# Linear attention into an ELU feed-forward: three steps of round four moved or recast (two decayed states to ScalarE, one decayed query sooner, two more ELU steps in SBUF form)

## The chip, the cores and the metric

The kernel runs on one core of one Trainium2 chip. The metric is device time in microseconds; less is better. One core has TensorE (matmuls, PE in the profile), VectorE (DVE), ScalarE (ACT), GpSimd (POOL) and SyncE (SP, here only a queue of DMA issues). Matmul results go to PSUM; everything else lies in SBUF.

## The reference, cut to what matters

Linear attention with a decay per head over q, k, v of shape 4 batches x 8 heads x 768 positions x 64, in blocks of 64 positions. Its output, laid out as 3072 rows of 512, goes through two matrix products with an ELU between them.

```python
for b in range(nb):                                   # 12 blocks of 64 positions
    intra = (qb @ kb.T) * Dmask                       # Dmask[i, j] = lam ** (i - j), causal
    out[:, :, sl] = intra @ vb + (qb * lam_pow) @ kv_state
    kv_state = lam_block * kv_state + (kb * rev_pow).T @ vb
h = x @ w_in                                          # 512 -> 2048
g = where(h > 0, h, exp(min(h, 0)) - 1)               # ELU
return g @ w_out                                      # 2048 -> 512
```

Inputs and the result are float32; the kernel works in float16 between them, with float32 sums in PSUM.

## The kernel before, in words

**Blocks.** Work is cut into 24 blocks numbered s = 0 to 23: block s is one step of 64 positions for a pair of batches, so blocks s and s - 2 are neighbours in time of the same pair. For a block the kernel makes: the decayed values vd (L191), the decayed state sd (L200: the state of block s - 2 times lam to the 64th, per head), the decayed queries qs (L209), the masked scores P (L217), the output cast xt (L252) and the new state st (L264: what PSUM holds plus sd). The transposed keys and queries T of blocks 10 and later come from two DMA transposes on SP's queue (`dma_T`, L234 to L243, tile TD, two buffers; the tile of block 13 is that of block 11, so its transposes wait until the scores and the decayed queries of block 11 have read it). qs has two buffers and sd three.

**A visit.** `visit` (L278) is the attention work of TensorE for several blocks at once: the visit of block s takes qs and the state to the inter-block part of block s (L304), the scores of block s + 1 (L328, from T), the state update of block s (L320, from vd) and the product with P of block s (L313). Then DVE makes P of block s + 1 and st of block s, and ACT casts the output of block s to xt.

**Rounds.** From round 3 on, a loop over rounds grp = 3 to 11 (L601) with eight steps u = 0 to 7 each sets the order. A step issues one feature product `mm1_h` (L377, L385: 16 matmuls for 256 rows, into one of two PSUM buffers psH) that is written H(grp,u) below. Blocks 2 grp + 2 and 2 grp + 3 are visited in steps 1 and 5, so round 4 visits blocks 10 and 11 and round 5 blocks 12 and 13. After a feature product comes a part of the second product of an earlier round (`part`, L508, or `mm2`, L452). The second product of round 3 and later is a Strassen-like scheme in seven products, whose sums of g are made by `g_sum` on DVE (L490), and whose one leftover weight sum is `w_sum(3, 1)` in step (5,0) (L478).

**The ELU.** `elu` (L420) has two forms. The SBUF form (`mm1_e`, `mm1_g`): ACT makes e = exp(psH) (L395) and r = relu(psH) in float16 (L397), and DVE makes g = min(e - 1, r) from these two (L402); the last reader of psH is ACT. The PSUM form: ACT makes r = relu(-psH) (L429) and e = exp(-r) (L431), and DVE makes g = max(e - 1, psH) (L432); the last reader of psH is DVE. Round 3 and steps 0 to 4 of round 4 take the SBUF form. Below, g(grp,u) is DVE's instruction of a step in either form.

**Order.** The schedule is written by hand: every engine runs its instructions in the order in which the program issues them, and only semaphores hold one back. The loads of k, q and v of a later block (L70, two DMA issues each) stand in POOL's queue, in steps 0 and 4 of a round. From block 12 on, POOL also makes qs and sd, in steps 1 and 5 (`decay_q(s + 1, ...)`, `decay_s(s + 1, ...)`, L616 and L617). For block 11 the loop does this on DVE apart: sd in step (4,2) after st of block 10 (L654), and qs in step (4,3) after vd of block 11 (L656).

Of the kernel before, what the change touches and what calls it, by code (L numbers as in the profile page):

```python
# [11 lines left out]
AF = mybir.ActivationFunctionType  # L12
# [4 lines left out]
def kernel(  # L17
# [10 lines left out]
    nc = tc.nc  # L28
# [3 lines left out]
    NPR = B // 2  # L32
    NHP = H // 2
# [134 lines left out]
    lamL = cst.tile([128, NHP], FP32, name="lamL")  # L168
    powi = cst.tile([128, NHP, L], FP32, name="powi")

    st = [dict() for _ in range(NS)]
    state = {}
# [23 lines left out]
    def decay_s(s, eng):  # L196
        if not NPR <= s < NS - NPR:
            return
        st[s]["sd"] = asb.tile([128, 2, NHP, D], FP32, tag="sd", bufs=3, name=f"sd{s}")
        eng.tensor_tensor(  # L200
            out=st[s]["sd"][:], in0=state[s - NPR][:],
            in1=lamL[:].unsqueeze(1).unsqueeze(3).broadcast_to([128, 2, NHP, D]), op=ALU.mult,
        )

    def decay_q(s, eng):
        if not NPR <= s < NS:
            return
        st[s]["qs"] = asb.tile([128, NHP, 2, L], FP16, tag="qs", bufs=2, name=f"qs{s}")
        eng.tensor_tensor(  # L209
            out=st[s]["qs"][:], in0=st[s]["T"][:, 1],  # L210
            in1=powi[:].unsqueeze(2).broadcast_to([128, NHP, 2, L]), op=ALU.mult,
        )
# [32 lines left out]
    def att_X(s, eng):  # L245
        g, hf = divmod(s, 2)
        if g not in xt:
            xt[g] = asb.tile([128, NHP, 256], FP16, tag="xt", bufs=3, name=f"xt{g}")
        to = xt[g][:, :, hf * 128 : (hf + 1) * 128].rearrange("p y (r t) -> p r y t", r=2)
        O = st[s].pop("O").rearrange("p r (y t) -> p r y t", y=NHP)  # L250
        if eng is nc.scalar:
            nc.scalar.copy(out=to, in_=O)  # L252
        else:
            eng.tensor_copy(to, O)
# [122 lines left out]
    def mm1_h(grp, c0, nc_, n0, step=1):  # L377

        T = nc_ * 128
        nb = 512 // T  # L380
        name = f"{grp}_{c0}_{n0}"
        psH = ps.tile([128, nb, T], FP32, tag="h", bufs=2, name=f"psH{name}")
        for i, n in enumerate(features(nb, n0, step)):
            for kk in range(NHP):
                nc.tensor.matmul(  # L385
                    psH[:, i, :], lhsT=wi[n // 4][:, kk, (n % 4) * 128 : (n % 4 + 1) * 128],
                    rhs=xt[grp][:, kk, c0 * 128 : c0 * 128 + T],
                    start=(kk == 0), stop=(kk == NHP - 1),
                )
        unit[grp, c0, nc_, n0] = (psH, nb, T, name)  # L390

    def mm1_e(grp, c0, nc_, n0):
        psH, nb, T, name = unit[grp, c0, nc_, n0]
        e = msb.tile([128, nb, T], FP32, tag="e", bufs=4, name=f"e{name}")
        nc.scalar.activation(e[:], psH[:], AF.Exp)  # L395
        r = msb.tile([128, nb, T], FP16, tag="r", bufs=4, name=f"r{name}")
        nc.scalar.activation(r[:], psH[:], AF.Relu)  # L397
        unit[grp, c0, nc_, n0] = (e, r, nb, T, name)

    def mm1_g(grp, c0, nc_, n0, step=1):  # L400
        e, r, nb, T, name = unit.pop((grp, c0, nc_, n0))
        nc.vector.scalar_tensor_tensor(  # L402
            out=place(grp, c0, nc_, n0, nb, step), in0=e[:], scalar=-1.0, in1=r[:],
            op0=ALU.add, op1=ALU.min,
        )

    def place(grp, c0, nc_, n0, nb, step=1):

        if grp not in gel:
            gel[grp] = msb.tile([128, NF2, 2, 256], FP16, tag="g", bufs=4, name=f"g{grp}")  # L410
        cols = slice(c0 * 128, (c0 + nc_) * 128)
        if step > 1:
            return gel[grp][:, n0, :, cols]
        return gel[grp][:, n0 % NF2 : n0 % NF2 + nb, n0 // NF2, cols]
# [5 lines left out]
    def elu(grp, u):  # L420

        psH, nb, T, name = unit[grp, 0, 2, u]
        if grp == 3 or grp == 4 and u < 5:
            mm1_e(grp, 0, 2, u)
            mm1_g(grp, 0, 2, u, NF2)
            return

        r = msb.tile([128, nb, T], FP32, tag="r", bufs=4, name=f"r{name}")
        nc.scalar.activation(r[:], psH[:], AF.Relu, scale=-1.0)  # L429
        e = msb.tile([128, nb, T], FP32, tag="e", bufs=4, name=f"e{name}")  # L430
        nc.scalar.activation(e[:], r[:], AF.Exp, scale=-1.0)  # L431
        nc.vector.scalar_tensor_tensor(  # L432
            out=place(grp, 0, 2, u, 2, NF2), in0=e[:], scalar=-1.0, in1=psH[:],
            op0=ALU.add, op1=ALU.max,
        )
# [11 lines left out]
    def mm2(s, n0):  # L447
        if n0 == 0:
            acc[s] = M[nacc[0] % 2][:]
            nacc[0] += 1  # L450
        for n in range(n0, n0 + 4):
            nc.tensor.matmul(  # L452
                acc[s], lhsT=g_of(s, n), rhs=wo[n // 4][:, n % 4, :],
                start=(n == 0), stop=(n == NFT - 1),
            )
# [145 lines left out]
    for grp in range(3, NG):  # L601
        old, new = grp - 2, grp - 1
        for u in range(8):
            mm1_h(grp, 0, 2, u, NF2)
            s = 2 * grp + 2 + u // 4
            if s < NS and u % 4 == 0:

                if nload < NS:
                    load("k", nload)
                    load("q", nload)  # L610
                if nload <= NS:
                    load("v", nload - 1)
                    nload += 1
            if s < NS and u % 4 == 1:
                if s != 10:
                    decay_q(s + 1, nc.vector if s < 10 else nc.gpsimd)  # L616
                    decay_s(s + 1, nc.vector if s < 10 else nc.gpsimd)  # L617
                visit(
                    s, s if s < NS - NPR else None, s + 1 if s + 1 < NS else None,
                    s + 2 if s + 2 < NT else None,  # L620
                )
                dma_T(s + 3)

            if (grp, u) in five:
                mm2(5, 4 * five.index((grp, u)))
            end = grp == NG - 1
            if old >= 3 and u in (0, 2):
                part(old, {0: 3, 2: 7}[u])
            if new >= 3:
                at_u = {1: 2, 3: 4, 4: 1, 5: 5, 6: 6, 7: 3} if end else {3: 2, 4: 1, 5: 4, 6: 5, 7: 6}  # L630
                if u in at_u:
                    part(new, at_u[u])

            if old >= 3 and u == 1:
                add(old, 0, hi, res[old]["A"][:, hi], "p35")
                store(2 * old, res[old][0], slice(0, DM))
            if old >= 3 and u == 0:
                g_sum(old, 3)
            if new >= 3 and u in (4, 5, 6):
                g_sum(new, {4: 1, 5: 2, 6: 4}[u])  # L640
            if end and u == 3:
                g_sum(new, 3)
            if new >= 3 and u == 4:
                add(new, 0, lo, res[new]["A"][:, hi], "p2")
            if s + 1 < NS:
                if u % 4 == 1:
                    att_P(s + 1)
                if u % 4 == 2:
                    att_C(s + 2)
                    att_N(s)  # L650
                if u in (3, 7) and grp > 3:
                    decay_v(s + 1, nc.vector)
                if (grp, u) == (4, 2):
                    decay_s(s + 1, nc.vector)  # L654
                if (grp, u) == (4, 3):
                    decay_q(s + 1, nc.vector)  # L656
            if old >= 3 and u == 2:
                c2(old)
            if (grp, u) == (5, 0):
                w_sum(3, 1)  # L660
            elu(grp, u)
            if grp == 3 and u in (3, 6):
                decay_v(s + 1, nc.vector)
            if s < NS and u % 4 == 1:
                att_X(s, nc.scalar)
            if old >= 3 and u == 0:
                keep(old, "p35", res[old]["B"][:, hi])
            if new >= 3 and u == (1 if end else 3):
                keep(new, "p2", res[new]["B"][:, lo])
            if new >= 3 and u == (5 if end else 6):  # L670
                keep(new, "c45", res[new]["B"][:])
            if end and u == 6:
                keep(new, "u2", res[new]["A"][:, hi], 1)
            if end and u == 7:
                add(new, 0, hi, res[new]["B"][:, hi], "u2")
                store(2 * new, res[new][0], slice(0, DM))
            if (grp, u) == five[-1]:
                mm2_o(5)
# [58 lines left out]
```

## Time and profile before

| what | value |
|---|---|
| device time, three runs | median 210.2 us (210.11 to 211.47) |
| profiled execution | 210.27 us, of which the span is 208.5 us |
| busy, share of the span | PE 190.2 us (91%), DVE 172.1 (83%), ACT 140.7 (68%), POOL 132.0 (63%) |
| granted TensorE clock | full in all 40 slices |
| length of rounds, H(grp,0) to H(grp+1,0) | 5: 14.69 us, 6: 14.70, 7: 15.00, 8: 14.70 |

Times in the rows are microseconds from the start of the span; a row of the timeline has start, duration, engine, line, operation, output <- inputs, shapes, count, and in brackets the idle time of the engine just before it with what ended that. Matmul durations overlap, so for TensorE starts are compared, not durations. DVE's and ACT's durations also overlap a little: a DVE instruction of 0.68 us is followed by the next 0.60 us after its start. Spans on POOL are rough.

### The profile page before, as it was taken

The page shows a single profiled execution, that of the slowest core. Times are in us where ns is not written, and L with a number is a line of the kernel's source. Part 1 is how long each engine was busy: PE and PEld are TensorE (multiplying, and loading weights), DVE is VectorE, ACT ScalarE, POOL GpSimd, SP SyncE. Part 2 cuts the span into 40 slices and gives each one's busy share as a digit, 9 for nine tenths or more (in the row PEclk, how much of TensorE's full clock was granted, in tenths as well). Part 3 has the DMA queues.
Part 4 walks back from the last instruction along what each step waited for, and adds up shares of the span by engine and source line. Part 5 has one row for each costly group of instructions (what it writes and reads, how often), then busy time and mean ns, then how long its engine had stood idle before and what let it go on. Part 6 is the DMA issues. An engine that isn't in the chain of part 4 may idle for free.

```text
span 208.5 us, 7848 instructions
## 1 busy us (share of the span) xinstructions
PE 190.2 (91%) x3352; PEld 158.1 (76%) x3352; DVE 172.1 (83%) x281; ACT 140.7 (68%) x265; POOL 132.0 (63%) x180
## 2 busy tenths in 40 slices
PE   0448989999999999989999999999999999999991
PEld 0347977846776777868888888888888888888880
DVE  3677596798989898999989999999979956758672
ACT  5314686741784878767878778778788688877820
POOL 8978933899899879964999999999412200000000
PEclk9999999999999999999999999999999999999999
DMA  6999999999999999999999999999924404004043
GB/s 103 145 152 134 169 200 196 179 118 170 109 148 153 168 115 162 114 74 108 126 170 90 151 163 72 190 116 91 189 29 57 101 0 105 5 6 94 3 101 101
DMA packets 99731, 24.38 MB, mean 117 GB/s; under 512 B 92400, under 2 KB 96752, under 8 KB 99696
## 3 DMA queue, kind: packets, MB, share of 16 engines
q0 software_dynamic: 78208, 13.38, 96.0%
q1 hardware_dynamic: 20128, 10.03, 25.5%
q10 hardware_dynamic: 1360, 0.46, 1.2%
q8 instruction: 26, 0.43, 0.8%
q14 instruction: 9, 0.07, 0.1%
HBM read 27.27 MB, written 6.29 MB: 161 GB/s over the span
## 4 chain that ended last, share of the span: by engine, by line
PE 83%; DVE 6%; POOL 3%; DMA 3%; issue 2%; ACT 1%; DVEq 0%; POOLq 0%
PE psH L385 40%; PE psM L508 22%; PE psM L452 10%; DMA wi<-in_moe_w_in_dram 3%; PE psO_None L304 2%; PE psZ L328 2%; POOL vn L70 1%; DVE g L432 1%; PE psO_None L313 1%; PE psHA L508 1%; PE psHB L508 1%; PE psZ L320 1%; DVE s L490 1%; DVE vd L191 1%; DVE P L217 1%
## 5 line engine op out<-in xcount | busy, mean ns | idle before, releaser
L385 PE MATMUL psH<-xt,wi 128*128 128x256 f16 (+1 forms) x960 | 101.8, 257 | 2.6 <-DMA wi<-in_moe_w_in_dram 1.7
L385 PEld LDWEIGHTS <-wi 128*128 128x128 f16 x960 | 80.7, 101 | 13.7 <-issue 2.7
L432 DVE SCALAR_TENSOR_TENSOR g<-e,psH 128x512 f16<-128x512 f32 x59 | 40.2, 682 | 12.5 <-ACT e L431 12.1
L429 ACT ACTIVATE r<-psH 128x512 f32<-128x512 f32 x59 | 35.2, 597 | 21.5 <-PE psH L385 21.4
L431 ACT ACTIVATE e<-r 128x512 f32<-128x512 f32 x59 | 37.2, 630 | 1.9
L70 POOL DMA_DIRECT2D qn<-in_q_dram x46 | 32.4, 727 | 5.3 <-issue 2.7
L70 POOL DMA_DIRECT2D vn<-in_v_dram x48 | 34.0, 734 | 2.6 <-DMA qn<-in_q_dram 1.0
L395 ACT ACTIVATE e<-psH 128x512 f32<-128x512 f32 x37 | 22.2, 599 | 19.1 <-PE psH L385 18.8
L70 POOL DMA_DIRECT2D kn<-in_k_dram x46 | 32.5, 725 | 2.3 <-DMA wo<-in_moe_w_out_dram 2.3
L508 PEld LDWEIGHTS <-s 128*128 128x128 f16 x288 | 28.1, 98 | 3.4
L402 DVE SCALAR_TENSOR_TENSOR g<-e,r 128x512 f16<-128x512 f32 x37 | 26.1, 713 | 5.2 <-ACT r L397 5.2
L209 POOL TENSOR_TENSOR qs<-TD,powi 128x512 f16<-128x512 f16 x12 | 15.8, 1316 | 17.3 <-PE psO_None L304 12.4
L508 PE MATMUL psM<-wt,s 128*128 128x256 f16 x192 | 24.9, 273 | 0.0
L452 PE MATMUL psM<-wo,g 128*128 128x512 f16 x96 | 23.9, 380 | 0.0
L508 PEld LDWEIGHTS <-g 128*128 128x128 f16 x216 | 20.5, 98 | 2.6
L397 ACT ACTIVATE r<-psH 128x512 f16<-128x512 f32 x37 | 22.1, 598 | 0.0
L191 DVE TENSOR_TENSOR vd<-vn,rev 128x512 f16<-128x512 f16 x22 | 19.6, 891 | 0.0
L217 DVE TENSOR_TENSOR P<-psZ,mask 128x512 f16<-128x512 f32 x24 | 16.4, 684 | 2.6 <-PE psZ L328 2.0
L508 PE MATMUL psM<-wo,g 128*128 128x256 f16 x136 | 17.6, 273 | 0.0
L252 ACT CAST xt<-psO_None 128x512 f16<-128x512 f32 x20 | 11.5, 577 | 6.2 <-PE psO_None L313 6.2
L264 DVE TENSOR_TENSOR st<-psZ,sd 128x512 f16<-128x512 f32 x20 | 13.7, 683 | 0.9 <-PE psZ L320 0.9
L200 POOL TENSOR_TENSOR sd<-st,lamL 128x512 f32<-128x512 f16 x10 | 13.4, 1345 | 1.4 <-DVE st L264 1.4
(77 smaller groups left out, 207.0 us busy)
## 6 DMA issues: line engine op xcount, KB each, us to landing
out_dram<-o SPq DMA_DIRECT2D x45, 128.0 KB, 3.4
vn<-in_v_dram POOLq DMA_DIRECT2D x48, 64.0 KB, 4.6
kn<-in_k_dram POOLq DMA_DIRECT2D x46, 64.0 KB, 4.5
qn<-in_q_dram POOLq DMA_DIRECT2D x46, 64.0 KB, 4.9
wi<-in_moe_w_in_dram POOLq DMA_DIRECT2D x8, 256.0 KB, 5.8
wo<-in_moe_w_out_dram POOLq DMA_DIRECT2D x4, 512.0 KB, 7.7
kraw<-in_k_dram SPq DMA_DIRECT2D x2, 128.0 KB, 4.1
qraw<-in_q_dram ACTq DMA_DIRECT2D x2, 128.0 KB, 4.5
```

The source lines that it names most:

```text
L70: nc.gpsimd.dma_start(out=keep[s][half(r)], in_=src[b + r, :, c * L : (c + 1) * L, :].rearrange("h p d -> p h d"),)
L191: eng.tensor_tensor(out=st[s]["vd"][:], in0=vn[s][:], in1=rev[:].unsqueeze(2).broadcast_to([128, H, D]), op=ALU.mult,)
L217: nc.vector.tensor_tensor(out=d["P"][:].rearrange("p y j t -> p y (j t)"), in0=psS, in1=mask[:].rearrange("p y j t -> p y (j t)"), op=ALU. ...
L385: nc.tensor.matmul(psH[:, i, :], lhsT=wi[n // 4][:, kk, (n % 4) * 128 : (n % 4 + 1) * 128], rhs=xt[grp][:, kk, c0 * 128 : c0 * 128 + T], s ...
L395: nc.scalar.activation(e[:], psH[:], AF.Exp)
L397: nc.scalar.activation(r[:], psH[:], AF.Relu)
L402: nc.vector.scalar_tensor_tensor(out=place(grp, c0, nc_, n0, nb, step), in0=e[:], scalar=-1.0, in1=r[:], op0=ALU.add, op1=ALU.min,)
L429: nc.scalar.activation(r[:], psH[:], AF.Relu, scale=-1.0)
L431: nc.scalar.activation(e[:], r[:], AF.Exp, scale=-1.0)
L432: nc.vector.scalar_tensor_tensor(out=place(grp, 0, 2, u, 2, NF2), in0=e[:], scalar=-1.0, in1=psH[:], op0=ALU.add, op1=ALU.max,)
L452: nc.tensor.matmul(acc[s], lhsT=g_of(s, n), rhs=wo[n // 4][:, n % 4, :], start=(n == 0), stop=(n == NFT - 1),)
L508: nc.tensor.matmul(to, lhsT=lhsT, rhs=rhs, start=start and n == 0, stop=stop and n == NF2 - 1, skip_group_check=True,)
```

## The change

Four edits, all about round 4:

- sd of block 11 is no longer made by DVE in step (4,2) but by ACT, after the ELU of step (4,4), as four activations (one per pair of heads, each of 128 x 128 elements) with the scale taken from a column of lamL.
- sd of block 12 is no longer made by POOL in step (4,5) but by ACT in the same way, after the cast of block 11's output in step (4,5).
- qs of block 11 stays on DVE and takes the place that sd of block 11 had, in step (4,2) instead of (4,3).
- Steps (4,5) and (4,6) take the SBUF form of the ELU, so seven steps of round 4 have it.

```diff
@@ decay_s(s, eng)
+        if eng is nc.scalar:
+
+            for j in range(NHP):
+                nc.scalar.activation(
+                    st[s]["sd"][:, :, j, :], state[s - NPR][:, :, j, :], AF.Copy,
+                    scale=lamL[:, j : j + 1],
+                )
+            return
@@ elu(grp, u)
-        if grp == 3 or grp == 4 and u < 5:
+        if grp == 3 or grp == 4 and u < 7:
@@ the loop over rounds
                 if s != 10:
                     decay_q(s + 1, nc.vector if s < 10 else nc.gpsimd)
+                if s not in (10, 11):
                     decay_s(s + 1, nc.vector if s < 10 else nc.gpsimd)
...
                 if (grp, u) == (4, 2):
-                    decay_s(s + 1, nc.vector)
-                if (grp, u) == (4, 3):
                     decay_q(s + 1, nc.vector)
...
             elu(grp, u)
+            if (grp, u) == (4, 4):
+                decay_s(11, nc.scalar)
             if grp == 3 and u in (3, 6):
                 decay_v(s + 1, nc.vector)
             if s < NS and u % 4 == 1:
                 att_X(s, nc.scalar)
+            if (grp, u) == (4, 5):
+                decay_s(12, nc.scalar)
```

## The prediction, made blind

> **What bounds the kernel now.** I read the page's chain first, then its stretches by round, then TensorE's own timeline where the chain leaves TensorE.
>
> ```profile
> span 208.5 us, 7848 instructions
> PE 83%; DVE 6%; POOL 3%; DMA 3%; issue 2%; ACT 1%; DVEq 0%; POOLq 0%
> 80.00:94.84 14.84, 13.70 (x234) 11.35 (x233) 14.21 (x22) 11.53 (x23) 11.81 (x15) 1.00 1.82 117
> 94.84:109.53 14.69, 14.69 (x250) 12.87 (x248) 14.05 (x23) 11.66 (x22) 12.87 (x15) 1.00 1.18 132
> 124.23:139.23 15.00, 14.86 (x250) 12.87 (x248) 14.60 (x22) 11.69 (x22) 15.00 (x18) 1.00 1.60 133
> ```
>
> The columns after the stretch are its length, then busy time of PE, PEld, DVE, ACT and POOL, the granted clock, the DMA share and GB/s. TensorE carries 83% of the chain and is busy for all 14.69 us of round 5, but only 13.70 of 14.84 us in the stretch that ends with round 4. DVE is nearly as full: 14.21 and 14.05 us. So the kernel is TensorE's sum, with DVE close behind; only TensorE's waits can be won. Around round 4 these are:
>
> ```profile
> 87.39 1.04 PE L385 MATMUL psH<-xt,wi 128*128 128x256 f16 x8
> 89.11 0.26 PE L304 MATMUL psO_None<-qs,st 64*64 64x64 f16 x8 [0.68 <-DVE qs L209]
> 91.56 1.04 PE L508 MATMUL psM<-wt,s 128*128 128x256 f16 x8
> 93.05 1.05 PE L385 MATMUL psH<-xt,wi 128*128 128x256 f16 x8 [0.46 <-DVE g L432]
> ...
> 95.71 1.04 PE L508 MATMUL psM<-wo,s 128*128 128x256 f16 x8
> 96.58 1.04 PE L385 MATMUL psH<-xt,wi 128*128 128x256 f16 x8
> 97.55 0.26 PE L304 MATMUL psO_None<-qs,st 64*64 64x64 f16 x8
> 98.25 1.05 PE L385 MATMUL psH<-xt,wi 128*128 128x256 f16 x8
> ```
>
> The rows are H(4,5), the visit of block 11, a part and H(4,7); then, a round on, an unheld part, H(5,1), visit and H(5,2). Unheld, a visit starts 0.97 us after its feature product (96.58 to 97.55); the visit of block 11 should have started at 88.36 and started at 89.11: 0.75 us lost to qs of block 11. Unheld, a feature product starts 0.87 after the part before it; H(4,7) should have started at 92.43 and started at 93.05: 0.62 lost to g(4,5), which held its psH. **Together 1.37 us**: all that these edits can win directly.
>
> **The change part by part.** DVE's queue in round 4 and what POOL does beside it:
>
> ```profile
> 84.75 0.68 DVE L200 TENSOR_TENSOR sd<-st,lamL 128x512 f32<-128x512 f16 x1
> 85.35 1.65 DVE L402 SCALAR_TENSOR_TENSOR g<-e,r 128x512 f16<-128x512 f32 x1
> 86.93 1.52 DVE L191 TENSOR_TENSOR vd<-vn,rev 128x512 f16<-128x512 f16 x1
> 88.38 0.68 DVE L209 TENSOR_TENSOR qs<-TD,powi 128x512 f16<-128x512 f16 x1
> 92.32 0.67 DVE L432 SCALAR_TENSOR_TENSOR g<-e,psH 128x512 f16<-128x512 f32 x1
> 84.87 1.59 POOL L209 TENSOR_TENSOR qs<-TD,powi 128x512 f16<-128x512 f16 x1 [0.17 <-DMA TD<-qn]
> 86.42 1.48 POOL L200 TENSOR_TENSOR sd<-st,lamL 128x512 f32<-128x512 f16 x1
> ```
>
> *Removed from DVE.* sd of block 11 takes one place, 0.60 us (84.75 to 85.35). g(4,2) and vd of block 11 take 1.65 and 1.52 us instead of 0.68: each ends 0.6 us after the end of the POOL instruction beside it (86.46, 87.90), so a DVE instruction with both inputs in SBUF is held until POOL's is over. sd of block 12 leaves POOL, and with it the hold of vd, 1.52 - 0.68 = 0.84 us. g(4,2) keeps its hold by qs of block 12. DVE wins 0.60 + 0.84 = 1.44 us.
>
> *qs one place sooner.* It runs at 84.75 and ends at 85.43. The visit then waits for vd of block 11: 86.93 + 0.68 = 87.61, before 88.36. In POOL's queue, though, the next loads move up to 86.42. Do loads hold DVE?
>
> ```profile
> 87.85 1.41 POOL L70 DMA_DIRECT2D kn<-in_k_dram  x2
> 90.57 1.41 POOL L70 DMA_DIRECT2D vn<-in_v_dram  x2
> 91.12 0.68 DVE L490 TENSOR_TENSOR s<-s,g 128x1024 f16<-128x1024 f16 x1
> 109.01 1.46 DVE L191 TENSOR_TENSOR vd<-vn,rev 128x512 f16<-128x512 f16 x1
> 109.03 1.41 POOL L70 DMA_DIRECT2D vn<-in_v_dram  x2
> ```
>
> Beside the first of six loads qs kept 0.68 at 88.38, beside the last a sum kept it at 91.12; a vd at 109.01, with loads of the same kind beside it, did not. So vd's hold by loads is 0 to 0.78 us; I take 0, as the rows of this same stretch say, and keep 0.78 for the range. Even so vd ends at 88.39, and 88.36 is nearly met. The Trainium skill, "SBUF — State Buffer", section "Who interferes with whom", says that a VectorE instruction with two SBUF inputs contends with a GpSimd instruction that reads SBUF, and infers that descriptor generation does not hold `tensor_tensor`. The 1.65 us row agrees; the row at 109.01, with only loads beside it, speaks against the inference. By the page alone vd's hold is 0, which is the value taken.
>
> *Seven steps in SBUF form.* psH of (4,5) is then freed by ACT, not at the end of g(4,5) (92.99). ACT has:
>
> ```profile
> 87.21 0.59 ACT L397 ACTIVATE r<-psH 128x512 f16<-128x512 f32 x1
> 90.07 0.58 ACT L252 CAST xt<-psO_None 128x512 f16<-128x512 f32 x1 [0.34 <-PE psO_None L313]
> 6.07 1.05 ACT L561 ACTIVATE powi<-i1f,loglamP 128x64 f32<-128x64 f32 x4
> L431 ACT ACTIVATE e<-r 128x512 f32<-128x512 f32 x59 | 37.2, 630 | 1.9
> L395 ACT ACTIVATE e<-psH 128x512 f32<-128x512 f32 x37 | 22.2, 599 | 19.1 <-PE psH L385 18.8
> ```
>
> *Four activations.* No row shows 128 x 128 with a scale column. Four of 128 x 64 take 1.05 us, four of 128 x 512 would take 4 x 0.63 = 2.5. Between these by elements (64 more of 448, of 1.5 us) I take 1.25 us. sd of block 11 fills 87.7 to 88.9 on ACT; H(4,5) ends at 88.4, so exp and relu of (4,5) run 88.9 to 89.9 and psH is free by 89.9, where H(4,7), 1.37 earlier, wants it at 91.68. At 2.5 us it is free at 91.2, still in time. The cast of block 11 follows, then sd of block 12 from 90.4 to 91.6, exp and relu of (4,6) to 92.6, needed by H(5,0) at 93.47; at 2.5 us each, all of ACT is 2.5 later there and costs up to 1.6 us. Block 11's sd is needed by DVE's st at 92.1 and block 12's a round later. ACT has the room: 11.53 of 14.84 us. Cost 0.
>
> *What is late next.* qs of block 11 was also what the transposes of block 13 waited for, and those what POOL waited for:
>
> ```profile
> 89.12 1.20 SPq L239 DMA_TRANSPOSE TD<-kn  x1
> 90.42 1.21 SPq L239 DMA_TRANSPOSE TD<-qn  x1
> 96.66 1.68 POOL L209 TENSOR_TENSOR qs<-TD,powi 128x512 f16<-128x512 f16 x1 [4.68 <-DMA TD<-qn]
> 98.30 1.03 POOL L200 TENSOR_TENSOR sd<-st,lamL 128x512 f32<-128x512 f16 x1
> 95.42 0.69 DVE L432 SCALAR_TENSOR_TENSOR g<-e,psH 128x512 f16<-128x512 f32 x1
> 96.03 0.68 DVE L490 TENSOR_TENSOR s<-g 128x1024 f16<-128x1024 f16 x1
> 96.63 0.69 DVE L478 TENSOR_TENSOR wt<-wo,wo 128x1024 f16<-128x1024 f16 x1
> 97.23 0.68 DVE L432 SCALAR_TENSOR_TENSOR g<-e,psH 128x512 f16<-128x512 f32 x1
> 149.68 1.16 POOL L209 TENSOR_TENSOR qs<-TD,powi 128x512 f16<-128x512 f16 x1 [2.57 <-PE psO_None L304]
> ```
>
> The transposes go out at about 85.5 and 86.8 and land, 6.2 us after the second as before (90.42 to 96.66), near 93.0. Before, POOL's qs and sd of block 13 stood beside PSUM readers of DVE (g<-psH here is not lengthened) and held nothing. Now they stand at 93 to 96, where DVE has g(4,6), now with two SBUF inputs, vd of block 12, a sum and the weight sum, all open to a hold.
>
> The sum, along DVE from 86.93 in places of 0.60 (0.34 for the half-width add): vd 86.93, g(4,3) 87.53, sum 88.13, add 88.73, g(4,4) 89.07, sum 89.67, P 90.27, g(4,5) 90.87, sum 91.47, st 92.07, g(4,6) 92.67 to 93.27. Here POOL's qs takes its turn for 1.16 (its row at 149.68): vd of block 12 runs at 94.4, not 93.3. POOL's sd takes 95.0 to 96.0; g(4,7), from PSUM, runs 95.0 to 95.7, and H(5,1), which wants to start at 96.58 - 1.37 = 95.21, starts at 95.7: 0.5 given back. The sum of step (5,0) is held to 96.0, weight sum at 96.6, g(5,0) at 97.2 to 97.9. Before it ran at 97.23 and H(5,2) followed 0.34 after its end; now H(5,2) follows at once, at 97.9 against 98.25. **Of 1.37 us, 0.35 is left** at H(5,2); the rest of DVE's gain is eaten by two holds of about 1 us.
>
> Later rounds differ only by where POOL stands. Round 7 is 0.31 us longer than round 5 (15.00 against 14.69), and TensorE idles in it; POOL, earlier against TensorE, may remove it or make another: 0 to 0.3 gained, a tenth taken. 210.27 - 0.35 - 0.1 = 209.8 us. The profiled execution is 208.5 of span and 1.77 around it, 0.07 above the median shown.
>
> **The rivals.**
>
> *Clean gain.* Transposes land so that qs and sd of block 13 fall beside g<-psH, st, P and the adds, or in front of DVE, which then makes POOL wait (POOL's 1.59 and 1.68 against 1.16). Then 1.37 us stays: 208.9; with round 7's 0.3, 208.6. For it: TensorE waits on nothing else in round 5. Against it: between 87 and 97 DVE now has only four or five instructions with a PSUM input.
>
> *Slower.* One mechanism, the holds of DVE by POOL between 86.4 and 97: beyond 1.44 + 0.34 = 1.78 us of holds, H(5,2) starts later than before. vd of block 11 held by loads (0.78), then qs of block 13 in front of a sum or g(4,6) (1.16) and sd in front of vd of block 12 (1.03) make 2.97: H(5,2) 1.2 later, 211.5. With half of the loads' hold and one of POOL's two cut to half, 2.1: 0.3 later, 210.6. For it: a landing can be shorter,
>
> ```profile
> TD<-qn SPq DMA_TRANSPOSE x1, 4.2
> ```
>
> is the one for block 14 (4.2 us from issue); at 4.2 qs of block 13 comes at 91.0, ahead of more open instructions. Against: DVE often goes first and POOL waits.
>
> *It doesn't do what it says.* The visit of block 11 waits for vd instead of qs, and H(4,7) for ACT instead of DVE: that takes activations of 2.5 us a set. Then H(5,0) waits until 92.6 + 2.5 = 95.1, and before it started 0.87 ahead of the part at 95.71, at 94.84: 0.3 slower, 210.5.
>
> **How the numbers follow.** Forecast case (0.1 to 0.8 won, 209.5 to 210.2): 0.42. Clean (208.6 to 209.4): 0.25. Slower (210.3 to 211.5): 0.25. No effect: 0.05; anything else, such as a hold that comes back in every round, 0.03. All of the named cases lie within 1%, which is about what this measurement can tell from no change. Beyond it on the fast side lies nothing that I can add up (1.37 + 0.3 is 0.8%); on the slow side a hold of 0.3 us in each of ten half rounds would do it (3 us). Faster 0.04, same 0.88, slower 0.08. The range leaves out the ends of the clean and the slow case: 208.7 to 210.9.
>
> **What would show it.** In the changed profile: no wait of TensorE for qs at the visit of block 11, none of psH L385 for g at H(4,7); vd of block 11 at 0.68; POOL's qs of block 13 at about 93 instead of 96.66; the longest DVE instructions of the stretch being vd of block 12 and the sum of step (5,0), at 1.2 to 1.8 us; a new wait of TensorE for g<-psH at H(5,1) or H(5,2). If H(5,2) starts near 96.9, the clean case holds; after 98.25, the slow one. The forecast is wrong if DVE is not held at 93 to 96, or if ACT's sets of four come out near 2.5 us.

## The result: 0.3 to 0.6% faster in three sets of runs, 0.2% forecast

| | before | changed |
|---|---|---|
| device time, median | 210.47 us (209.28 to 213.31, 20 runs) | 209.43 us (207.5 to 211.31, 20 runs) |
| ratio, 95% interval | 1 | 0.994 (0.9913 to 0.9967) |
| profiled execution | 210.27 us, span 208.5 | 209.93 us, span 208.1 |
| two more sets of runs, ratio | 1 | 0.997 (0.9935 to 1.0005) and 0.9951 (0.9916 to 0.9986) |

209.8 us was forecast, a gain of 0.45, and 208.7 to 210.9 given as the range. In three sets of runs the median lies 1.04, 0.43 and 0.91 us (0.2 to 0.5%) under that of before, and the ratios are 0.3 to 0.6% under 1; the interval of the second set reaches 1. Ratios and intervals are of the fast runs alone, which leave out those more than 1.5% above the fastest of their kernel. The profiled execution lies 0.5 us above its kernel's median.

The page of the changed kernel, its chain, and one of its rounds (the columns are those of the stretches shown before: length, PE, PEld, DVE, ACT, POOL):

```profile
span 208.1 us, 7855 instructions
PE 87%; POOL 4%; DMA 3%; DVE 2%; issue 1%; ACT 0%; DVEq 0%; POOLq 0%
80.15:93.58 13.43, 13.43 (x235) 11.36 (x234) 12.80 (x20) 12.97 (x30) 12.53 (x18) 1.00 2.24 150
93.58:109.56 15.98, 14.91 (x251) 12.94 (x249) 15.17 (x24) 11.90 (x23) 14.04 (x19) 1.00 1.51 122
109.56:124.25 14.69, 14.69 (x250) 12.88 (x248) 12.71 (x22) 11.70 (x22) 12.79 (x17) 1.00 1.36 136
```

DVE's share of the chain fell from 6% to 2%. TensorE is now busy for the whole of the stretch up to H(5,0), 13.43 of 13.43 us, and idle for 1.07 us in the next, 14.91 of 15.98. So the waits of round 4 were won, and most of what they cost was lost again at the start of round 5. TensorE's rows there are H(4,5), the visit of block 11, H(4,7), H(5,0), H(5,1), the visit of block 12 and H(5,2):

```profile
87.54 1.04 PE L393 MATMUL psH<-xt,wi 128*128 128x256 f16 x8
88.51 0.26 PE L312 MATMUL psO_None<-qs,st 64*64 64x64 f16 x8
91.83 1.04 PE L393 MATMUL psH<-xt,wi 128*128 128x256 f16 x8
93.58 1.04 PE L393 MATMUL psH<-xt,wi 128*128 128x256 f16 x8
96.48 1.03 PE L393 MATMUL psH<-xt,wi 128*128 128x256 f16 x8 [1.00 <-DVE g L440]
97.45 0.26 PE L312 MATMUL psO_None<-qs,st 64*64 64x64 f16 x8
98.28 1.03 PE L393 MATMUL psH<-xt,wi 128*128 128x256 f16 x8
```

The visit comes 0.97 us after H(4,5) and H(4,7) 4.29 us after it (before 5.66): both waits are gone, 1.37 us. Then H(5,1) waits 1.00 us for g(4,7). The reason stands on DVE and POOL:

```profile
86.11 0.68 DVE L191 TENSOR_TENSOR vd<-vn,rev 128x512 f16<-128x512 f16 x1
87.31 1.65 DVE L498 TENSOR_TENSOR s<-g 128x1024 f16<-128x1024 f16 x1
92.82 2.41 DVE L410 SCALAR_TENSOR_TENSOR g<-e,r 128x512 f16<-128x512 f32 x1
95.16 0.68 DVE L191 TENSOR_TENSOR vd<-vn,rev 128x512 f16<-128x512 f16 x1
95.76 0.67 DVE L440 SCALAR_TENSOR_TENSOR g<-e,psH 128x512 f16<-128x512 f32 x1
92.44 1.24 POOL L217 TENSOR_TENSOR qs<-TD,powi 128x512 f16<-128x512 f16 x1
93.57 1.10 POOL L208 TENSOR_TENSOR sd<-st,lamL 128x512 f32<-128x512 f16 x1
```

POOL's queries and state of block 13, which stood at 96.66 and 98.30 before, are at 92.44 and 93.57. g(4,6) started during the first and ended at 95.23, 0.56 us after the second was over (94.67): it waited 1.73 us, through both.

**How the traces are compared.** H(4,5) is the last milestone that the change didn't move: in every trace below it comes 5.07 or 5.08 us after the visit of block 10, which stands ahead of the first changed instruction. H(4,5) itself came at 85.8 to 88.9 us, and in the three traces of the changed kernel alone at 87.54, 88.50 and 87.14. That scatter of up to 3 us is larger than what the kernels differ by afterwards. So every trace is read from its own H(4,5) on, in us, to its last instruction:

| kernel | H(4,7) | H(5,1) | H(5,2) | end | ratio of medians |
|---|---|---|---|---|---|
| before | 5.66 | 9.19 | 10.86 | 121.07 | 1 |
| changed, three traces | 4.29 | 8.94, 8.43, 8.81 | 10.74, 10.23, 10.61 | 120.61, 120.11, 120.48 | 0.994, 0.997, 0.995 (intervals above) |
| ELU form alone | 5.04 | 8.66 | 10.46 | 120.95 | 1.001 (0.997 to 1.005) |
| queries sooner alone | 5.66 | 9.93 | 11.66 | 121.53 | 1.002 (0.998 to 1.005) |
| changed, ELU form undone | 4.29 | 8.31 | 10.12 | 120.00 | 0.993 (0.989 to 0.996) |
| changed, block 12's state on POOL | 4.29 | 9.01 | 10.81 | 120.69 | 1.003 (0.999 to 1.007) |
| changed, loads first | 4.29 | 7.78 | 13.53 | not compared | 0.996 (0.991 to 1.000), from five of twelve runs |
| block 13's state on ScalarE | 4.29 | 7.78 | 9.44 | 120.09 | 0.993 (0.989 to 0.996) |
| ... and block 13's queries on DVE | 4.29 | 7.78 | 9.44 | 120.08 | 0.989 (0.984 to 0.993) |
| block 13's state on DVE late, two traces | 4.29 | 7.78, 7.87 | 9.45, 9.67 | 119.53, 119.76 | 0.990 (0.986 to 0.994), 0.992 (0.988 to 0.995) |
| the same, ELU form undone | 4.29 | 8.03 | 9.72 | 119.85 | 0.994 (0.991 to 0.998) |

In the trace with the loads first TensorE ran at 0.6 of its clock in a slice after H(5,2), so its end is left out.

### The profile page after: what moved, and what is told of

It reads as the page before. It is cut to its first block, busy times and chain, and to the rows that moved or that the text cites. A ratio compares the mean times of both kernels' runs of the same rounds, so it can differ in the third digit from the quotient of the medians.

```text
span 208.1 us, 7855 instructions
## 1 busy us (share of the span) xinstructions
PE 190.1 (91%) x3352; PEld 158.2 (76%) x3352; DVE 167.5 (80%) x280; ACT 142.4 (68%) x273; POOL 127.4 (61%) x179
## 4 chain that ended last, share of the span: by engine, by line
PE 87%; POOL 4%; DMA 3%; DVE 2%; issue 1%; ACT 0%; DVEq 0%; POOLq 0%
PE psH L393 42%; PE psM L516 24%; PE psM L460 10%; DMA qn<-in_q_dram 3%; PE psO_None L312 3%; PE psZ L336 2%; POOL vn L70 1%; PE psO_None L321 1%; POOL kn L70 1%; PE psZ L328 1%; PE psHA L516 1%; PE psHB L516 1%; PE psO L343 1%; POOL qn L70 1%; POOL wi L88 1%
## 5 line engine op out<-in xcount | busy, mean ns | idle before, releaser
L440 DVE SCALAR_TENSOR_TENSOR g<-e,psH 128x512 f16<-128x512 f32 x57 | 39.0, 684 | 16.2 <-ACT e L439 15.6
L437 ACT ACTIVATE r<-psH 128x512 f32<-128x512 f32 x57 | 34.1, 598 | 19.7 <-PE psH L393 19.6
L439 ACT ACTIVATE e<-r 128x512 f32<-128x512 f32 x57 | 35.9, 630 | 1.8
L403 ACT ACTIVATE e<-psH 128x512 f32<-128x512 f32 x39 | 23.3, 599 | 18.8 <-PE psH L393 18.5
L410 DVE SCALAR_TENSOR_TENSOR g<-e,r 128x512 f16<-128x512 f32 x39 | 28.2, 730 | 6.0 <-ACT r L405 5.9
L405 ACT ACTIVATE r<-psH 128x512 f16<-128x512 f32 x39 | 23.3, 598 | 0.0
L217 POOL TENSOR_TENSOR qs<-TD,powi 128x512 f16<-128x512 f16 x12 | 14.6, 1217 | 12.6 <-PE psO_None L312 12.4
L191 DVE TENSOR_TENSOR vd<-vn,rev 128x512 f16<-128x512 f16 x22 | 15.0, 683 | 0.0
L208 POOL TENSOR_TENSOR sd<-st,lamL 128x512 f32<-128x512 f16 x9 | 9.4, 1047 | 8.1 <-DVE st L272 8.1
```

The source lines that it names most:

```text
L191: eng.tensor_tensor(out=st[s]["vd"][:], in0=vn[s][:], in1=rev[:].unsqueeze(2).broadcast_to([128, H, D]), op=ALU.mult,)
L410: nc.vector.scalar_tensor_tensor(out=place(grp, c0, nc_, n0, nb, step), in0=e[:], scalar=-1.0, in1=r[:], op0=ALU.add, op1=ALU.min,)
L440: nc.vector.scalar_tensor_tensor(out=place(grp, 0, 2, u, 2, NF2), in0=e[:], scalar=-1.0, in1=psH[:], op0=ALU.add, op1=ALU.max,)
```

## The experiments

The theory: the change removes TensorE's two waits, and POOL, whose work on block 13 is set free 4 us sooner, takes most of it back by holding DVE. The rivals: the ELU form carries the gain; ScalarE is what is late at H(5,1); the gain is only the scatter of the first 88 us.

**The ELU form alone.** The kernel before with

```diff
-        if grp == 3 or grp == 4 and u < 5:
+        if grp == 3 or grp == 4 and u < 7:
```

> The kernel before with one edit: steps (4,5) and (4,6) take the SBUF form of the ELU; both decayed states and the decayed queries stay as before. Theory (waits and holds): the wait of TensorE for the queries of block 11 stays (about 0.7 us), the wait of H(4,7) for g(4,5) (0.62) goes; POOL's queries of block 13 stay late (about 96.6), so nothing holds g(4,6) and 0.4 to 0.6 us is won: ratio 0.997 to 0.998. Rival (the whole change wins by the state moves alone): H(4,7) then waits for ACT or the gain is lost again by H(5,2), ratio 1.000.

H(4,7) came 5.04 us after H(4,5): the wait of 0.62 for psH is gone, that of 0.7 for the queries of block 11 stays, as expected. H(5,2) is 0.40 earlier, the end only 0.12: 0.4 to 0.6 us were expected, and most of what was won is lost again in round 6, which took 14.93 us instead of 14.70. The medians can't tell it from before. So the form removes its own wait, and no gain from it alone is shown.

**The moves alone.** The changed kernel with u < 5 again in that line.

> The changed kernel with one edit undone: steps (4,5) and (4,6) back in PSUM form. Theory: DVE is 1.4 us earlier, so the visit of block 11 and H(4,7) are on time without the new form; POOL's queries and state of block 13 at 92 to 95 now hold vd of block 12 instead of g(4,6), and H(5,1) still waits 0.3 to 1.0 us for g(4,7). Ratio to before 0.995 to 0.998, as the changed kernel or a little worse. Rival (the ELU form carries the gain): H(4,7) waits again by about 0.6 us for g(4,5), ratio 0.999 to 1.001.

```profile
95.02 1.52 DVE L191 TENSOR_TENSOR vd<-vn,rev 128x512 f16<-128x512 f16 x1
93.83 1.16 POOL L217 TENSOR_TENSOR qs<-TD,powi 128x512 f16<-128x512 f16 x1 [1.80 <-DMA TD<-qn]
94.96 1.03 POOL L208 TENSOR_TENSOR sd<-st,lamL 128x512 f32<-128x512 f16 x1
```

These are DVE and POOL of that run. g(4,6), reading PSUM, wasn't held; vd of block 12 was, by the state of block 13, to 0.55 us after its end. H(4,7) is on time without the form, against the rival. The end, 120.00, is 0.1 us ahead of the best of the changed kernel's three, and the ratio, 0.993, lies under the 0.995 to 0.998 expected; on the same chip the changed kernel had 0.997. So beside these moves the two more steps in SBUF form were not needed for the gain.

**The queries alone.** The kernel before with the two instructions of DVE in each other's place:

```diff
                 if (grp, u) == (4, 2):
-                    decay_s(s + 1, nc.vector)
-                if (grp, u) == (4, 3):
                     decay_q(s + 1, nc.vector)
+                if (grp, u) == (4, 3):
+                    decay_s(s + 1, nc.vector)
```

> The kernel before with one edit: the decayed queries and the decayed state of block 11 change places on DVE (queries in step (4,2), state in (4,3)); both decayed states stay where they were and the ELU forms too. Theory: the visit of block 11 waits only for vd, 0.1 us instead of 0.75, but DVE's sum up to g(4,5) is the same, so H(4,7) comes 5.6 to 5.7 us after H(4,5) as before: nothing won there. The transposes of block 13 go out earlier, POOL's queries and state of block 13 now fall on vd of block 12 and the sums, and H(5,2) comes 0.2 to 1.0 us later than before (11.1 to 11.9 after H(4,5)): slower. Rival (the visit's wait is worth its 0.75 us): H(5,2) at 10.1 to 10.3.

TensorE and DVE of that run:

```profile
93.02 1.05 PE L385 MATMUL psH<-xt,wi 128*128 128x256 f16 x8 [1.20 <-DVE g L432]
95.55 1.03 PE L385 MATMUL psH<-xt,wi 128*128 128x256 f16 x8 [0.61 <-DVE g L432]
92.88 1.42 DVE L490 TENSOR_TENSOR s<-g,s 128x1024 f16<-128x1024 f16 x1
95.42 1.15 DVE L191 TENSOR_TENSOR vd<-vn,rev 128x512 f16<-128x512 f16 x1
```

The visit's wait went and H(4,7) waited 1.20 instead of 0.46: 5.66 us after H(4,5), to the hundredth what it was. What TensorE wins at one wait it spends at the next as long as DVE's sum is the same. Then a sum and vd of block 12 were held, both unheld before, and H(5,2) came 0.80 later; the medians don't show this loss (1.002, from 0.998 to 1.005). The other half of the theory is seen here without the ELU form or ScalarE having any part.

**Block 12's state back on POOL.** The changed kernel with

```diff
-                if s not in (10, 11):
+                if s != 10:
...
-            if (grp, u) == (4, 5):
-                decay_s(12, nc.scalar)
```

> The changed kernel with block 12's decayed state back on POOL (block 11's stays on ScalarE). Read from H(4,5), since the first 88 us differ by up to 3 us between executions whatever the kernel. Theory (holds): vd of block 11 is held again (about 1.5 us), DVE is 0.8 us later than in the changed kernel; H(4,7) is still on time, 4.3 us after H(4,5) (before: 5.66), because ScalarE frees its psH; H(5,2) comes 10.7 to 11.3 us after H(4,5) (before 10.86, changed 10.2 to 10.7): most of the gain is gone. Rival (what matters is DVE's one instruction less and the earlier queries, not the hold of vd): H(5,2) at 10.2 to 10.7 as in the changed kernel.

Against the expectation vd was not held (0.68 us); the queries of block 11 (1.34) and g(4,2) (1.52) were, by POOL's queries and state of block 12. H(5,2) at 10.81 lies in the expected band and only 0.07 after the worst of the changed kernel. The median says slower or the same, the trace a gain of 0.38 at the end: this one edit's worth stays open within about 0.5 us.

**Loads first.** The loads of step (5,4) go out in step (5,0), so that POOL has six more issues ahead of the queries of block 13:

```diff
-            if s < NS and u % 4 == 0:
+            for _ in range({(5, 0): 2, (5, 4): 0}.get((grp, u), 1) if s < NS and u % 4 == 0 else 0):
```

> The changed kernel with the loads of step (5,4) issued in step (5,0) already, ahead of POOL's queries and state of block 13, so that these start about 4.1 us later (near 96.6 instead of 92.4), as before the change. Theory (two POOL instructions back to back hold g(4,6) for 1.7 us and so H(5,1) for 1.0): g(4,6) takes 0.68 us, H(5,1) starts without a wait, about 1.1 us earlier, and H(5,2) keeps 1.0 us or more of it: ratio to before 0.991 to 0.994. Rival (g(4,6) is late for another reason, ACT or the loads' descriptors): g(4,6) stays at 1.5 us or more, or the wait moves to H(5,2), ratio as the changed kernel, 0.994 to 0.996.

```profile
93.92 4.85 DVE L486 TENSOR_TENSOR wt<-wo,wo 128x1024 f16<-128x1024 f16 x1
94.80 1.31 POOL L217 TENSOR_TENSOR qs<-TD,powi 128x512 f16<-128x512 f16 x1
95.92 1.17 POOL L208 TENSOR_TENSOR sd<-st,lamL 128x512 f32<-128x512 f16 x1
96.92 1.29 POOL L217 TENSOR_TENSOR qs<-TD,powi 128x512 f16<-128x512 f16 x1
```

Half of it held: g(4,6) took 0.68 us and H(5,1) came at 7.78, without a wait. But the expectation missed what stands behind: with no loads left between them, the queries of block 14 followed the state of block 13 at once, and the weight sum took 4.85 us, to 0.56 us after the third POOL instruction in a row. H(5,2) waited 4.02, for the g behind it. Not all of the hold is explained: the weight sum started 0.88 us ahead of the first of the three, beside a load of POOL, and unheld would have been over by then. As the rival had it, the wait moved to H(5,2). This execution took 212.74 us, near the median of all twelve runs (212.43), while the ratio of 0.996 rests on the five shortest; how long the hold is in those isn't known. A clean gain was not had, but by this one trace a hold can last through three POOL instructions.

**Block 13's state on ScalarE.** The changed kernel with a third set of four activations, after the cast of step (5,1), and none of it on POOL:

```diff
-                if s not in (10, 11):
+                if s not in (10, 11, 12):
...
+            if (grp, u) == (5, 1):
+                decay_s(13, nc.scalar)
```

> The changed kernel with block 13's decayed state on ScalarE too (after the cast of step (5,1)), so that POOL has one instruction, the queries of block 13, at 92 to 95 instead of two. Theory: DVE is held once, by at most 1.2 us; H(5,1) comes 7.8 to 8.3 us after H(4,5) (unheld 7.82, changed 8.4 and 8.9), H(5,2) 9.5 to 10.1. Rival (ScalarE has no room for a third set): g of step (5,2) waits for it and H(5,4) comes late by 0.5 us or more.

ScalarE, DVE and TensorE of that run:

```profile
97.98 1.27 ACT L203 ACTIVATE sd<-st,lamL 128x128 f32<-128x128 f16 x4
92.77 1.05 DVE L410 SCALAR_TENSOR_TENSOR g<-e,r 128x512 f16<-128x512 f32 x1
100.43 0.69 DVE L440 SCALAR_TENSOR_TENSOR g<-e,psH 128x512 f16<-128x512 f32 x1 [0.84 <-ACT e L439]
101.17 1.05 PE L393 MATMUL psH<-xt,wi 128*128 128x256 f16 x8 [0.57 <-DVE g L440]
```

g(4,6) was held once, to 1.05, and H(5,1) had no wait at all; H(5,2) at 9.44 keeps the whole 1.37. The rival of ScalarE holds too, two steps later: its third set makes g(5,2) late by 0.84 and H(5,4) by 0.73. The end, 120.09, is no better than the changed kernel's best.

**No POOL tensor instruction at block 13.** As the last, and the queries of block 13 on DVE:

```diff
-                    decay_q(s + 1, nc.vector if s < 10 else nc.gpsimd)
+                    decay_q(s + 1, nc.vector if s < 10 or s == 12 else nc.gpsimd)
```

> The changed kernel with block 13's queries on DVE (step (5,1)) and block 13's state on ScalarE, so that POOL has only loads between the queries of block 12 and those of block 14. Theory: no DVE instruction between 89 and 97 takes over 0.8 us; H(5,1) comes 7.8 us after H(4,5), H(5,2) 9.5 to 9.7, the whole 1.37 us kept; ratio to before 0.990 to 0.993, the best of the kernels. Rival (loads hold DVE as well, or the next POOL queries, of block 14, fall earlier and hold it by H(5,4)): the gain is lost again by H(6,0), ratio as the changed kernel.

No DVE instruction from 88 to 97 took over 0.7 us, H(5,2) came at 9.44. The loads that POOL issued there held nothing. But H(5,3) and H(5,4) came 0.3 and 0.7 us late (11.49 and 13.68 after H(4,5), against 11.20 and 12.95 in the next kernel), with ScalarE's third set. The ratio, 0.989, is the lowest of all, from six runs, but the trace gives 120.08 from H(4,5) to the end, hardly under the changed kernel's best. This trace, the fastest run of its set, reached H(4,5) at 85.78, the earliest of all; whether an early start is behind the ratio too isn't shown.

**The state of block 13 on DVE, late.** The changed kernel with that state off POOL and ScalarE, in a step where DVE sat idle for ScalarE:

```diff
-                if s not in (10, 11):
+                if s not in (10, 11, 12):
...
+                if (grp, u) == (5, 5):
+                    decay_s(s, nc.vector)
```

> The changed kernel with block 13's decayed state taken off POOL as before, but put on DVE in step (5,5), where DVE waits 0.5 us for ScalarE, instead of on ScalarE. Theory: as with that state on ScalarE, DVE is held once at 92 to 95 and H(5,2) comes 9.4 to 9.7 us after H(4,5); and ScalarE has no third set, so H(5,4) follows H(5,2) after 3.5 us (4.2 there). From H(4,5) to the end 119.2 to 119.6 us (before 121.1, changed 120.1 and 120.6). Rival (DVE has no room in step (5,5) either): g(5,5) or g(5,6) comes late, H(5,7) or H(6,0) waits 0.3 to 0.6, from H(4,5) to the end 119.9 to 120.2.

H(5,2) at 9.45, H(5,4) 3.50 later, the end at 119.53: 1.08 us ahead of the first trace of the changed kernel, 0.58 of its best, and 1.54 of before. The cost of the new place shows as 1.30 us of DVE in step (5,5), held by POOL, and 0.12 us at H(5,7) and H(6,0) together. With the ELU form undone in this kernel:

> As the kernel with block 13's state on DVE in step (5,5), but with the SBUF form of the ELU in five steps of round 4 only, as before the change. Theory (the two more steps are worth nothing once DVE is 1.4 us earlier): H(4,7) 4.3 us after H(4,5), H(5,2) 9.4 to 10.0, from H(4,5) to the end 119.2 to 119.9 us; g(4,6) cannot be held in this form, vd of block 12 can. Rival (the form is needed, since DVE then is what frees psH): H(4,7) or H(5,0) waits 0.2 to 0.6 us for g and the end comes at 119.9 to 120.4.

H(5,0) waits 0.24 us for g(4,6), which then frees psH (6.28 us after H(4,5) against 6.04), H(5,2) comes at 9.72 and the end at 119.85, against 119.53 and 119.76 in two traces with the form. So once the holds are gone, the two steps in SBUF form are worth 0.1 to 0.3 us by these single traces; with the holds no worth shows.

**Both on one chip.** The changed kernel twice more, the second time on one chip with the kernel that has the state on DVE:

> The changed kernel once more, for the same chip as the three others and a second trace. Theory: g(4,6) again stands beside POOL's queries and state of block 13 and is held for 0.5 to 1.8 us, by where the transposes of block 13 land in that execution; H(5,1) waits 0.2 to 1.1 us. Ratio 0.992 to 0.997. If g(4,6) is not held here, the 1.0 us in the first trace is one draw and not the rule.

> The changed kernel, on one chip with the best version, as its yardstick and as a third trace. Theory: H(4,7) 4.3 us after H(4,5), DVE held by two POOL instructions at 92 to 96 for 1.0 to 1.8 us in all, H(5,2) 10.1 to 10.8 us after H(4,5), from H(4,5) to the end 120.0 to 120.6. If the end comes before 119.8, the holds of the first two traces were not the rule.

> Block 13's state on DVE in step (5,5), beside the changed kernel on one chip. Theory: H(5,2) 9.4 to 9.7 us after H(4,5), from H(4,5) to the end 119.4 to 119.8, and a median 0.4 to 1.0 us under that of the changed kernel. Rival (the difference of 0.6 to 1.0 us seen in the traces is lost in what differs before H(4,5)): medians within 0.3 us.

The second and the third trace of the changed kernel, two rows of DVE and two of POOL from each:

```profile
93.78 1.05 DVE L410 SCALAR_TENSOR_TENSOR g<-e,r 128x512 f16<-128x512 f32 x1
94.75 1.52 DVE L191 TENSOR_TENSOR vd<-vn,rev 128x512 f16<-128x512 f16 x1
93.05 1.23 POOL L217 TENSOR_TENSOR qs<-TD,powi 128x512 f16<-128x512 f16 x1 [1.41 <-PE psM L516]
94.25 1.48 POOL L208 TENSOR_TENSOR sd<-st,lamL 128x512 f32<-128x512 f16 x1
```

```profile
92.42 1.43 DVE L410 SCALAR_TENSOR_TENSOR g<-e,r 128x512 f16<-128x512 f32 x1
93.77 1.52 DVE L191 TENSOR_TENSOR vd<-vn,rev 128x512 f16<-128x512 f16 x1
92.05 1.24 POOL L217 TENSOR_TENSOR qs<-TD,powi 128x512 f16<-128x512 f16 x1
93.19 1.56 POOL L208 TENSOR_TENSOR sd<-st,lamL 128x512 f32<-128x512 f16 x1
```

In both, DVE got in between the two POOL instructions and was held twice: 0.37 and 0.84 us, and 0.75 and 0.84 us, where the first trace has one hold of 1.73. The 0.37 of g(4,6) is less than the 0.5 to 1.8 expected of it. H(5,1) waited for g(4,7) in all three, 0.48 to 1.00 us. The holds are the rule; their sum, 1.2 to 1.7 us, differs from execution to execution. When DVE gets in between is open: g(4,6) started 0.38 us after POOL's queries in the first trace, where it didn't, and 0.37 after them in the third, where it did. In the last set the medians were 210.52 (before), 209.61 (changed, 0.9951) and 208.66 (state on DVE, 0.9917, interval 0.9879 to 0.9954): 0.95 us between the last two, with 0.72 between their traces from H(4,5) on. Both point the same way: block 13's state late on DVE is better than the change, though the two intervals against before overlap.

## Why the prediction was right

The time alone confirms no mechanism: the range was 2.2 us wide, and the median, 209.43, lies between the forecast case and the clean one. The traces tell them apart.

**The two waits: exact.** 1.37 us was read off TensorE's rows; every trace of the changed kernel has H(4,7) 1.37 us sooner after H(4,5).

**DVE's 1.44 us: right in the sum.** g(4,6) was forecast to start 5.28 us after H(4,5), and did so in all three traces. vd of block 11 took 0.68 us, not held by loads, the value taken. The hold by the queries of block 12 stayed and moved, in the first trace to a sum (1.65).

**ScalarE's cost: right.** Sets of four took 1.27 to 1.30 us against 1.25, and nothing in round 4 waited for them. The room was smaller than "11.53 of 14.84" made it look: a third set cost 0.73 us.

**The loss to POOL: right in mechanism and size, wrong in place.** The term that was mis-sized is the landing. The transposes went out at 85.65 and 86.94 (forecast 85.5 and 86.8), but the second landed 5.2 us after its issue, and 5.0 and 5.3 in the other two traces, where 6.2 was taken. So POOL's queries of block 13 started 4.90, 4.55 and 4.91 us after H(4,5) instead of 5.61, and thus ahead of g(4,6) at 5.28 instead of behind it. In the first and the third trace it was not even the landing that POOL waited for last, but its own loads, the last of which ends where the queries begin:

```profile
91.08 1.41 POOL L70 DMA_DIRECT2D vn<-in_v_dram  x2
```

The sum had two holds of about 1 us, on vd of block 12 and on the sum of step (5,0), the second behind g(4,7). In the traces all of the hold falls ahead of g(4,7), on g(4,6) alone or on g(4,6) and vd of block 12, and the sum of step (5,0) was never held. So H(5,1) lost 1.16, 0.65 and 1.03 instead of 0.5, and H(5,2) little more. The forecast kept 0.35 of the 1.37 at H(5,2); the three traces kept 0.12, 0.63 and 0.25, in the mean 0.33. With a scatter of 0.5 and the holds in other places than in the sum, it is partly luck that the mean comes so close.

**Later rounds: the term that was too small.** Of the 0 to 0.3 us that round 7 might give, a tenth was taken; the runs show the whole. From H(5,2) to the end before has 110.21 us and the changed kernel 109.87, 109.88 and 109.87: 0.34, of which 0.31 is round 7 (14.69 in all three traces, 15.00 before). Before, H(7,1) came 2.06 us after H(7,0) at 124.23 (1.75 in the changed kernel), right behind a g that was late because vd ahead of it was held by POOL's queries:

```profile
123.84 1.24 POOL L209 TENSOR_TENSOR qs<-TD,powi 128x512 f16<-128x512 f16 x1
124.05 1.59 DVE L191 TENSOR_TENSOR vd<-vn,rev 128x512 f16<-128x512 f16 x1
125.56 0.67 DVE L432 SCALAR_TENSOR_TENSOR g<-e,psH 128x512 f16<-128x512 f32 x1
126.29 1.03 PE L385 MATMUL psH<-xt,wi 128*128 128x256 f16 x8
```

In the changed kernel that vd takes 0.69. The kernel with the queries sooner alone has 109.87 from H(5,2) on, that with the ELU form alone 110.49, so the gain comes from the sooner queries. In sum the traces gain 0.46, 0.96 and 0.59 us, 0.67 in the mean against 0.45 forecast; the medians of the three sets give 1.04, 0.43 and 0.91. There is one trace of before, so the last tenths stay open.

**The rivals.** The clean gain, H(5,2) 9.4 to 9.7 us after H(4,5), is seen only where one or both of POOL's instructions for block 13 are taken off the stretch. The slower case came out for the queries alone, 0.46 us slower to the end by its trace, which its medians don't show. The case of no effect needed sets of 2.5 us on ScalarE, and they took 1.3. That the gain is only scatter of the first 88 us doesn't fit: read from H(4,5) on, all three traces are ahead of before.

## What to carry to other kernels

An instruction moved forward also moves what waits for it on other engines: here two DMA transposes, and behind them two POOL instructions that then stood beside DVE instructions that they hold. Where an engine in order has its sum nearly full, a removed wait pays only what is also taken out of that engine's sum; here the same move without it gained nothing. Where starts scatter by more than the effect, read the traces from the last milestone that the change can't have moved.

## What the runs showed of the hardware

**A hold doesn't end with one instruction.** DVE, with both inputs in SBUF, waited through two POOL tensor instructions (2.41 us) that followed each other at once, and in other executions of the same program got in between (1.05 and 1.52). Beside three in a row one trace has 4.85 us, 0.88 of it ahead of the first, beside a load; the same weight sum beside the same load took 0.68 in the kernel without POOL instructions for block 13. The Trainium skill, "SBUF — State Buffer", section "SBUF: two separate sides", gives the shared pair of ports to whoever starts first for the whole instruction; the holds of 1.52 fit, and that a waiting DVE can miss the change of instructions is beyond what it says.

**A POOL that is late holds DVE far more than one on time.** From 98 to 150 us DVE had 12 instructions over 0.75 us in the trace of before and one, of 0.82, in each of the three of the changed kernel, with the same work on both engines. DVE's busy time in round 6 fell from 14.70 us to the 12.71 of the row above, POOL's from 14.70 to 12.79. What differs is what POOL waits for, before and then changed, each between 92 and 152 us (waits in total, how many, the longest):

```profile
POOL qs L209 <- DMA TD<-qn: 4.7, 1, 4.7
POOL qs L209 <- PE psO_None L304: 2.6, 1, 2.6
```

```profile
POOL sd L208 <- DVE st L272: 8.1, 8, 1.4
POOL qs L217 <- PE psO_None L312: 2.6, 1, 2.6
```

Before, POOL lost 4.7 us to the transposes of block 13 and from then on ran back to back, its tensor instructions wherever they fell. Now it waits for st in eight half rounds, so its state starts right behind a DVE instruction, beside readers of PSUM. The kernel with the queries sooner alone shows no DVE instruction over 0.75 us after 100 us, and that with the ELU form alone again has twelve. Not all twelve are held by tensor instructions of POOL: four of those before, at 101.41, 109.01, 116.10 and 121.56, took 1.05 to 1.46 us and would, unheld, have ended beside loads alone. Why loads hold DVE there and not beside vd of block 11 is open. TensorE was the bound there in both, so the 2 us less of DVE in a round were worth 0.34 us in all.
